# A fused attention and mixer block in fp32 by high and low parts: six plain chunks and 24 groups in place of eight and 20, with W4's low part made by DMA

## The chip, the cores and the metric

The kernel runs on one core of one Trainium2 chip. The metric is the device time of one launch in microseconds (us); the median of three runs is given, and the profile comes from one further execution. The engines are TensorE (PE), ScalarE (ACT), VectorE (DVE), GpSimd (POOL) and SyncE (SP). Each works off its own instructions in the order in which they stand and waits only by semaphores. SP and POOL issue the DMAs; in this kernel the accumulating ones (destination += source) are all issued by POOL.

## The reference, cut to what matters

```python
xn = _layernorm(x)                                  # x: 2048 tokens x 576
return x + _A_ref(xn, A_wqkv, A_wo) + _B_ref(xn, B_w1, B_w2, B_w3, B_w4)

# _A_ref: 32 heads of 18, each token sees 8 keys at distances 0, 2, .., 14
logits = einsum("bhsd,bhswd->bhsw", q, kg) * scale
o = einsum("bhsw,bhswd->bhsd", softmax(logits), vg)
return o.reshape(B, S, D) @ wo

# _B_ref: a mixer with shifted channel groups, then an MLP with F = 4608
hs = concatenate([g0, g1, g2, g3]) @ w2
x1 = x + hs
return x1 + _gelu(_layernorm(x1) @ w3) @ w4
```

All of it is float32.

## The kernel before, in words

**Precision.** A float32 operand is split into a high part, rounded to the PE's fp32r format, and a low part, the rest. A product is then three matmul passes (high x high, high x low, low x high). `PAIRS` lists the 14 passes of a 576-long contraction; `HALVES` the 7 passes of a 288-long one.

**Stages.** First qkv, spilled to DRAM (`qkvd`), then the mixer with w1 and w2, and x1 in the buffer `Y` (16 token tiles of 128 tokens). Then comes the MLP, which is two thirds of the span, and last the attention's output projection with `Wo`.

**The MLP** runs over pairs of 128-wide pieces of F. A pair is called a chunk here; there are 18.

- The first `NPL` = 8 chunks are *plain*. A unit is one chunk with one block of 512 tokens (L960): `up` makes two hidden pieces (2 x 14 matmuls of 512 columns), GELU follows on ACT, `low_part` on DVE takes the low part, and during the next unit `down` (L830) multiplies them by W4 for four token tiles (12 matmuls of 288 columns each). That is 32 units.
- The other 10 chunks run in *groups* (L1140). A group is one chunk with 1024 tokens. The two halves of the contraction, of the tokens and of the chunk form a 2 x 2 matrix product which is made with seven products (`P1` to `P7`, 7 x 7 matmuls of 512 columns) out of sums of the operands and weights. Beside the products stand eight token tiles of `down`, `D0` to `D7`, which belong to the group before. The order of these 15 items is written out by hand (`ORDER`, L1135, with other orders for the first group and for the two at the passage between the first and the second half of the tokens, `q = NWP - 1` and `q = NWP`). `at(item, f)` puts side work behind an item. There are 20 groups; group 0 also finishes the downs of the last unit.

**What a product waits for.** The products of one group share a few PSUM banks: a bank `ca` is copied by ACT after P1 (`keep(Z1, ca)`), continues to accumulate with P6, is copied again (`keep(Z2, ca)`), continues with P7 and so on (L1262 to L1286). PE may not write on before ACT's copy is done.

**Weights of a group.** `load_pair` (L915) loads w3's raw pieces into one buffer `w3st` with six DMAs; `split_a` writes the pieces for three products into `w3a`, `combine` forms sums in `w3st`, and `split_s` writes those for the other four into `w3s`. Each `split` has two ACT passes, one small accumulating DMA on POOL and one DVE pass. The next `load_pair` can start only when all readers of `w3st` are done.

**Weights W4.** `load_w4` (L554) loads 256 rows raw into the slots of token tiles 1 and 3 of `Y`. `split_w4` (L562) makes the high part on ACT (L566) and the low part on DVE (L569). Two such tiles exist.

**Token sums.** A `down` result is added to its token tile. For the ten tiles in `YD` (L34) the sum lies in DRAM: ACT copies PSUM into a staging buffer (L846) and POOL issues an accumulating DMA (L847). Their slots in `Y` are free for other use (staging, scratch, raw weights). For the other six DVE adds in `Y` (L851).

**The operands of the groups** are sums and differences of blocks of the normalised x1, loaded with `get_op` and split with `split_op` (three ACT passes L902 to L904, two DVE passes). At the passage between the token halves all seven are loaded and split anew.

**The attention** itself (scores, softmax, weighted sum) runs on DVE in the background. It is a Python generator that yields a cost after each instruction; `bg` takes pieces from it: 9.4 us per unit from unit 4 on, and in a group 1.6 us per item less what `spent` counts for other DVE work. The heads are cut into eight parts. A part's output is summed in the first half of the buffer `po` and stored to DRAM (`od`, L719). All must be done at item P4 of the sixth group from the end, where its memory is given up.

Of the kernel before, what the change touches and what calls it, by code (L numbers as in the profile page):

```python
# [17 lines left out]
NT = S // 128  # L18
# [15 lines left out]
YD = (1, 2, 3, 5, 7, 9, 10, 11, 13, 15)  # L34


NPL = 8
# [20 lines left out]
def fused_block(ctx, tc, x, wqkv, wo, w1, w2, w3, w4, out):  # L58
# [511 lines left out]

    x1n = {}
# [105 lines left out]
    def attention(ap):  # L677
# [8 lines left out]
        o = po[:, 0, :].rearrange("p (x d) -> p x d", d=HD)  # L686
# [12 lines left out]
        def av(g):  # L699
            if g == NG - 1:  # L700
                exp_now()
            L, v = Ls[g], vs[g]
            Lf = L.rearrange("p j h w -> p (j h) w")
            dve.tensor_reduce(den[g], Lf, axis=AX.X, op=ALU.add)
            dve.reciprocal(den[g], den[g])
            yield 0.8
            dve.tensor_tensor(Lf, Lf, den[g][:, :, None].to_broadcast([128, TPP * GH, W]),
                              op=ALU.mult)
            yield 0.6
            for w in range(W):  # L710
                vv = v[:, DIL * w:DIL * w + TPP, :].rearrange("p j (h d) -> p (j h) d", d=HD)
                dst = prod if w else o
                dve.tensor_tensor(dst, vv, Lf[:, :, w:w + 1].to_broadcast([128, TPP * GH, HD]),  # L713
                                  op=ALU.mult)
# [4 lines left out]
            sp.dma_start(od.rearrange("(p j) d -> p j d", p=128)[:, :, g * GC:(g + 1) * GC],  # L719
                         po[:, 0, :].rearrange("p (j c) -> p j c", c=GC))  # L720
# [242 lines left out]
    RATE = [9.4, 0.0]  # L963
# [6 lines left out]
    for u, (c, b) in enumerate(units):  # L970
# [6 lines left out]
        z = u - NU  # L977
        if z == -2:
            rtemps[:] = [2, 13, 15]
        r = 0.0 if u < 4 else (RATE[0] if z < -2 else RATE[1]) / 6  # L980
        for i in range(C):
# [11 lines left out]
            if (u, i) == (3, 0):  # L993
                pool.dma_start(yd[13], Y[:, 13, :])
                pool.dma_start(yd[15], Y[:, 15, :])
# [15 lines left out]
        for j, (t, parts) in enumerate(prev):  # L1011
# [24 lines left out]
        if z == -5:  # L1036
            load_pair(0)
        if z == -3:
# [5 lines left out]
        if z == -2:  # L1044
# [10 lines left out]
        if 14 <= u < 14 + NT:  # L1055
            add_x(u - 14)
# [83 lines left out]
    for q in range(NQ):  # L1140
# [4 lines left out]
        if q == 0:  # L1145
            rtemps[:] = [2]
        if z == -1:
            evc_pool.__exit__(None, None, None)
            opc.__exit__(None, None, None)
            EV[0] = (9, 11, 10, 2)  # L1150
# [26 lines left out]
        if q == 0:  # L1177
            at("P2", split_op, 0, "B22")
            at("P5", split_op, 0, "T4")
            at("P7", split_a, n, (0, 1))  # L1180
            at("D1", gelu22)
            at("D1", split_a, n, (2,))
            at("D2", low22)
            at("P3", combine, n)
# [4 lines left out]
            at("D3", split_w4, p)  # L1189
            at("D3", load_pair, q + 2)  # L1190
        elif q == NWP - 1:
            rtemps[:] = [2, 13]
# [10 lines left out]
            at("D2", split_w4, p)  # L1203
# [3 lines left out]
        elif q == NWP:  # L1207
            rtemps[:] = [2]
# [12 lines left out]
        elif z < -1:  # L1221
# [4 lines left out]
            at("D3", split_w4, p, 0)  # L1226
            at("P4", gelu22)
            at("P4", split_w4, p, 1)
# [7 lines left out]
        else:  # L1236
            at("D3", split_w4, p)
# [23 lines left out]
        for it in ORDERS.get(q, ORDER).split():  # L1261
# [29 lines left out]
            if z < -6 or z == -6 and EV[0]:  # L1291
                bg(1.6 - spent[0], it == "P6" and q != NWP - 1)
# [21 lines left out]
    for j in range(8):  # L1314
        tiles[j]()
        if j == 0:
            low_part(h21, Z4)
            load_y((1, 2, 3, 5))
            EV[0] = (9, 11, 10, 15, 13)
# [15 lines left out]
    for t in range(NT):  # L1335
# [6 lines left out]
        if t == 3:  # L1342
            load_y((9, 10, 11, 13, 15))
# [48 lines left out]
```

## Time and profile before

| what | us |
|---|---|
| median of 3 runs | 1292.73 (1290.86 to 1295.98) |
| profiled execution, its own time | 1294.18 |
| its span | 1292.4 |
| PE busy | 1267.1 |
| DVE busy | 944.7 |
| ACT busy | 598.7 |
| POOL busy | 246.3 |

Busy time is a sum over instructions; issuing a DMA from SP is not counted. The span by stages: from 399.6 to 718.6 us the plain units from the eighth on run, from there to about 1215 the groups, then the last downs and the output projection. In rows of waits, "A <- B: total, times, longest" is the time that A stood because B was not done. In rows of a timeline, the first two numbers are start and length in us, and the bracket at the end is the idle time before and what ended it.

### The profile page before, as it was taken

What the parts mean: (1) busy time and instruction counts of PE and PEld (TensorE: products, weight loads), DVE (VectorE), ACT (ScalarE), POOL (GpSimd) and SP (SyncE); (2) the same over time, 40 slices, a digit from 0 to 9 for tenths busy, and PEclk for the clock granted to TensorE, in tenths of its full rate; (3) what the DMA queues carried; (4) which work ended last, traced back from release to release, by engine and by line L of the source; (5) the groups of instructions that cost most, each with busy time, mean ns of one, the idle gap of its engine ahead of it and who ended that gap; (6) DMA issues with size and microseconds to landing.
All of it is one profiled execution on the core that took longest, in us unless ns stands there. A gap on an engine that the chain in (4) does not pass through costs nothing.

```text
span 1292.4 us, 19686 instructions
## 1 busy us (share of the span) xinstructions
PE 1267.1 (98%) x7538; PEld 1163.1 (90%) x7538; DVE 944.7 (73%) x1261; ACT 598.7 (46%) x952; POOL 246.3 (19%) x358
## 2 busy tenths in 40 slices
PE   8999999999999999999999999999979999999999
PEld 8999998899898998999999799989968999988998
DVE  6456534778469999999999789989978554566542
ACT  3322126526634434343345746546547555555530
POOL 2011100021221212231212212222212222222100
PEclk9999999999999999999999999999989999999999
DMA  7646874246886878989788767686595757799972
GB/s 210 156 113 139 171 173 143 73 131 174 220 245 148 180 165 202 229 154 222 136 200 204 168 136 163 112 191 154 106 261 87 155 102 154 178 218 222 254 250 83
DMA packets 201374, 219.16 MB, mean 170 GB/s; under 512 B 79152, under 2 KB 137744, under 8 KB 201152
## 3 DMA queue, kind: packets, MB, share of 16 engines
q1 hardware_dynamic: 168912, 151.57, 40.9%
q0 software_dynamic: 32368, 66.34, 32.2%
q8 instruction: 59, 0.97, 0.3%
q14 instruction: 35, 0.29, 0.1%
HBM read 119.73 MB, written 107.28 MB: 176 GB/s over the span
## 4 chain that ended last, share of the span: by engine, by line
PE 74%; DMA 8%; issue 7%; DVE 6%; ACT 2%; SPq 2%; POOL 1%; DVEq 0%; POOLq 0%; ACTq 0%
PE ps L842 26%; PE ps L214 16%; PE cc L1075 12%; PE p L823 12%; PE ps L466 4%; PE ps L313 3%; DMA yd<-Y 2%; DMA w3st<-in_B_w_dram 1%; DMA Y<-in_B_w_dram 1%; DMA w3a<-w3st 1%; DVE w L569 1%; DMA od<-po 1%; PE ps L481 1%; DVE w3st L931 1%; DMA w3s<-w3st 1%
## 5 line engine op out<-in xcount | busy, mean ns | idle before, releaser
L842 PEld LDWEIGHTS ps<-w,c 128*128 128x128 f32 x3456 | 474.9, 188 | 28.1 <-DVE Y L851 7.7
L842 PE MATMUL ps<-w,c 128*128 128x288 f32 x3456 | 486.4, 295 | 11.9 <-DVE Y L851 5.6
L847 POOL DMA_DIRECT2D yd<-Y x154 | 137.3, 897 | 453.9 <-ACT Y L846 378.6
L846 ACT COPY Y<-ps 128x576 f32<-128x576 f32 x154 | 98.1, 637 | 141.8 <-PE ps L842 90.4
L817 DVE TENSOR_TENSOR c<-Y,c 128x512 fp32r<-128x512 f32 x144 | 98.5, 685 | 60.0 <-ACT Y L806 49.9
L214 PE MATMUL ps<-WQ,xt 128*128 128x432 f32 x672 | 134.8, 360 | 0.0
L214 PEld LDWEIGHTS ps<-WQ,xt 128*128 128x128 f32 x672 | 125.6, 188 | 5.7
L851 DVE TENSOR_TENSOR Y<-ps,Y 128x576 f32<-128x576 f32 x108 | 81.1, 751 | 48.8 <-PE ps L842 48.5
L1075 PE MATMUL cc<-xt,w3s 128*128 128x512 f32 x420 | 108.8, 400 | 0.0
L737 DVE TENSOR_TENSOR po<-q,k 128x2304 f32<-128x2304 f32 (+1 forms) x40 | 82.9, 2073 | 16.1 <-issue 10.9
L805 ACT ACTIVATE c<-p 128x512 fp32r<-128x512 f32 x64 | 38.3, 599 | 119.3 <-PE p L823 119.3
L1075 PEld LDWEIGHTS cc<-xt,w3s 128*128 128x128 f32 x420 | 77.4, 192 | 14.1 <-DVE Y L1085 0.2
L740 DVE TENSOR_REDUCE L<-po 128x128 f32<-128x2304 f32 (+1 forms) x40 | 82.7, 2068 | 0.4
L1081 ACT COPY Y<-cc 128x512 f32<-128x512 f32 x60 | 35.1, 585 | 100.7 <-PE cc L1075 94.9
L121 POOL TENSOR_TENSOR rs<-rs,mhalf 128x1 f32<-128x1 f32 x48 | 31.6, 659 | 258.1 <-DVE rs L120 147.8
L717 DVE TENSOR_TENSOR po<-po 128x1152 f32<-128x1152 f32 x56 | 75.8, 1353 | 0.9
L713 DVE TENSOR_TENSOR po<-v,L 128x1152 f32<-128x1152 f32 x56 | 75.6, 1352 | 0.7
L323 ACT COPY stg<-ps 128x864 f32<-128x864 f32 x24 | 21.2, 882 | 102.8 <-PE ps L214 55.8
L1075 PE MATMUL cc<-x1n,w3a 128*128 128x512 f32 (+1 forms) x280 | 67.9, 393 | 0.0
L1075 PEld LDWEIGHTS cc<-x1n,w3a 128*128 128x128 f32 (+1 forms) x280 | 51.6, 188 | 10.3
L214 PE MATMUL ps<-W,h 128*128 128x288 f32 x384 | 53.5, 295 | 0.0
L823 PE MATMUL p<-xt,w3s 128*128 128x512 f32 x224 | 52.4, 390 | 0.0
(189 smaller groups left out, 1904.3 us busy)
## 6 DMA issues: line engine op xcount, KB each, us to landing
yd<-Y POOLq DMA_DIRECT2D x156, 288.0 KB, 5.3
Y<-in_B_w_dram SPq DMA_DIRECT2D x27, 576.0 KB, 6.9
w3st<-in_B_w_dram SPq DMA_DIRECT2D x52, 256.0 KB, 6.4
qkvd<-stg SPq DMA_DIRECT2D x24, 432.0 KB, 3.5
yd<-ev POOLq DMA_DIRECT2D x26, 288.0 KB, 6.2
xd<-st SPq DMA_DIRECT2D x16, 320.0 KB, 6.0
xd<-big SPq DMA_DIRECT2D x16, 320.0 KB, 7.9
w3st<-in_B_w_dram SPq DMA_DIRECT2D x76, 64.0 KB, 6.6
```

The source lines that it names most:

```text
L214: pe.matmul(ps[:, h, :n], xs(a), ws(b, h), start=i == 0, stop=i == len(PAIRS) - 1)
L713: dve.tensor_tensor(dst, vv, Lf[:, :, w:w + 1].to_broadcast([128, TPP * GH, HD]), op=ALU.mult)
L717: dve.tensor_tensor(o, o, dst, op=ALU.add)
L737: dve.tensor_tensor(dst, qf[:, None, :].to_broadcast([128, n, TPP * GC]), win, op=ALU.mult)
L740: dve.tensor_reduce(Lw[:, w:w + n, :], dst.rearrange("p w (x d) -> p w x d", d=HD), axis=AX.X, op=ALU.add)
L817: dve.tensor_tensor(h[:, 1, :], g, h[:, 0, :].bitcast(F32), op=ALU.subtract)
L823: pe.matmul(ps, W3[f][:, w, :], x1n[b][:, a, :], start=n == 0, stop=n == len(PAIRS) - 1)
L842: pe.matmul(ps[:, k, :HF], h[:, col], w[:, p, k * HF:(k + 1) * HF], start=n == 0, stop=n == len(seq) - 1)
L846: act.copy(e.rearrange("p (h c) -> p h c", h=2), ps[:, :, :HF])
L847: pool.dma_start(yd[t], e, accum_op=ALU.add)
L851: dve.tensor_tensor(yv, ps[:, :, :HF], yv, op=ALU.add)
L1075: pe.matmul(ps, WX[w][:k, v, SLOT[w], :], area[sb][xk][:k, a, :], start=onto is None and i == 0, stop=last and i == len(HALVES) - 1, skip_ ...
```

## The change

Six things change together; nothing that is computed does.

1. `NPL` is 6: 24 units and 24 groups.
2. `YD` has twelve tiles: 6 and 14 are summed in DRAM too. Their slots become scratch (6) and a further staging buffer (14).
3. In groups, and for the first group's W4, `split_w4g` takes the place of `split_w4`. ACT writes the negated raw value, rounded, into the low part's place; an accumulating DMA on POOL, within SBUF, adds the raw value; a second ACT pass writes the high part. DVE has no part in it.
4. The first group's W4 is loaded at the end of the fourth unit from the end of the plain stage and split in the unit after it. Before, it was loaded at the end of the second from the end and split at D3 of group 0.
5. In group 0, `split_a` of the next weights goes from behind P7 to behind P1, `combine` from P3 to D2.
6. The last of the attention's eight parts puts its output into the buffer of its q. The background budget in groups is 1.45 us per item and the rate in one late unit 5.0; x is added to the tiles seven units earlier.

```diff
-YD = (1, 2, 3, 5, 7, 9, 10, 11, 13, 15)
-NPL = 8
+YD = (1, 2, 3, 5, 6, 7, 9, 10, 11, 13, 14, 15)
+NPL = 6
...
+    def split_w4g(c, step=None):
+        t = W4["pair", c]
+        raw = Y[:, 0:4, :].rearrange("p (a b) c -> p a b c", b=2)[:, :, 1, :]
+        if step != 1:
+            act.activation(t[:, :, 1, :], raw, AF.Identity, scale=-1.0)
+            pool.dma_start(t[:, :, 1, :].bitcast(F32), raw, accum_op=ALU.add)
+        if step != 0:
+            act.copy(t[:, :, 0, :], raw)
...
+            o, out = (o_, po[:, 0, :]) if g < NG - 1 else (
+                qs[g].rearrange("p j (h d) -> p (j h) d", d=HD), qs[g].rearrange("p j d -> p (j d)"))
...
-    RATE = [9.4, 0.0]
+    RATE = [9.4, 5.0, 0.0]
+    BUDGET = 1.45
...
+        if u == 4:
+            EV[0] = (9, 11, 10, 14)
         if z == -2:
-            rtemps[:] = [2, 13, 15]
-        r = 0.0 if u < 4 else (RATE[0] if z < -2 else RATE[1]) / 6
+            rtemps[:] = [2, 6, 13, 15]
+        r = 0.0 if u < 4 else (RATE[0] if z < -3 else RATE[1] if z < -2 else RATE[2]) / 6
...
-            for f in {(-3, 1): (lambda: split_a(0),), (-3, 3): (lambda: combine(0),),
+            for f in {(-3, 1): (lambda: split_a(0),), (-3, 2): (lambda: split_w4g(NPL),), (-3, 3): (lambda: combine(0),),
...
+        if z == -4:
+            load_w4(NPL)
...
-            load_w4(NPL)
...
-        if 13 <= u < 13 + NT:
-            load_xa(u - 13)
+        if 6 <= u < 6 + NT:
+            load_xa(u - 6)
...
         if q == 0:
+            at("P1", split_a, n, (0, 1))
             at("P2", split_op, 0, "B22")
+            at("P6", split_a, n, (2,))
             at("P5", split_op, 0, "T4")
-            at("P7", split_a, n, (0, 1))
             at("D1", gelu22)
-            at("D1", split_a, n, (2,))
             at("D2", low22)
-            at("P3", combine, n)
+            at("D2", combine, n)
...
-            at("D3", split_w4, p)
...
-            at("D2", split_w4, p)
+            at("D2", split_w4g, p)
...
-            at("D3", split_w4, p, 0)
+            at("D3", split_w4g, p, 0)
             at("P4", gelu22)
-            at("P4", split_w4, p, 1)
+            at("P4", split_w4g, p, 1)
...
-            at("D3", split_w4, p)
+            at("P7", split_w4g, p)
...
-                bg(1.6 - spent[0], it == "P6" and q != NWP - 1)
+                bg(BUDGET - spent[0], it == "P6" and q != NWP - 1)
```

Three places in the engines' orders. The first is ACT in group 0, from the copy after P1 (`Y<-cc`, the buffer Z1) on. The xt rows are the split of operand B22, the second `Y<-cc` is the copy after P6, c the GELU of the next hidden piece; w3a comes from the buffer `w3st`. Before:

```order
L1081 COPY Y<-cc_6674 128x512
L902 ACTIVATE xt<-xt 128x1024
L903 ACTIVATE Y<-xt 32x512
L904 ACTIVATE xt<-xt 64x512
L1081 COPY Y<-cc_6674 128x512
L811 ACTIVATE c_6735<-Y 128x512
```

And with the change:

```order
L1097 COPY Y<-cc_5809 128x512
L947 CAST w3a<-w3st 128x768
L949 ACTIVATE w3a<-w3st,kv 96x384
L913 ACTIVATE xt<-xt 128x1024
L914 ACTIVATE Y<-xt 32x512
L915 ACTIVATE xt<-xt 64x512
L1097 COPY Y<-cc_5809 128x512
```

The two passes that write w3a stood behind the third copy of the bank; they now stand ahead of the second.

The second place is POOL's queue over one group of the first token half (yd are the stores of token tiles, w3a and w3s the small DMAs of the splits, w the low part of W4). Before:

```order
L847 DMA yd_86<-Y 128x576
L847 DMA yd_87<-Y 128x576
L847 DMA yd_88<-Y 128x576
L847 DMA yd_89<-Y 128x576
L939 DMA w3a<-w3st 32x384
L847 DMA yd_90<-Y 128x576
L939 DMA w3s<-w3st 32x512
```

And with the change:

```order
L858 DMA yd_86<-Y 128x576
L858 DMA yd_87<-Y 128x576
L858 DMA yd_88<-Y 128x576
L858 DMA yd_89<-Y 128x576
L950 DMA w3a<-w3st 32x384
L858 DMA yd_90<-Y 128x576
L858 DMA yd_91<-Y 128x576
L576 DMA w_6205<-Y 128x2x576
L950 DMA w3s<-w3st 32x512
```

A sixth tile and the whole low part of W4 stand ahead of the small DMA that ends the reading of `w3st`.

The third is ACT at the passage between the token halves (group `NWP - 1`), from the split of the second operand (x1n) to the copy of tile D3 (`Y<-ps`) and the first splits after it. Before:

```order
L902 ACTIVATE x1n_6402<-x1n_6402 128x1024
L903 ACTIVATE Y<-x1n_6402 32x512
L904 ACTIVATE x1n_6402<-x1n_6402 64x512
L566 CAST w_8665<-Y 128x2x576
L846 COPY Y<-ps_8810 128x576
L811 ACTIVATE c_8825<-Y 128x512
```

And with the change:

```order
L857 COPY Y<-ps_8393 128x576
L913 ACTIVATE x1n_5537<-x1n_5537 128x1024
L914 ACTIVATE Y<-x1n_5537 32x512
L915 ACTIVATE x1n_5537<-x1n_5537 64x512
L575 ACTIVATE w_8270<-Y 128x2x576
L578 CAST w_8270<-Y 128x2x576
L857 COPY Y<-ps_8416 128x576
```

The copy of D2 (the first row) is new, since tile 6 is now summed in DRAM, and W4 has two passes there.

More of the change, by code (lines that the diff above doesn't have):

```diff
@@ L719, in av @@
             sp.dma_start(od.rearrange("(p j) d -> p j d", p=128)[:, :, g * GC:(g + 1) * GC],
-                         po[:, 0, :].rearrange("p (j c) -> p j c", c=GC))
+                         out.rearrange("p (j c) -> p j c", c=GC))
         yield None
@@ L994, in fused_block @@
                 pool.dma_start(yd[13], Y[:, 13, :])
+                pool.dma_start(yd[14], Y[:, 14, :])
                 pool.dma_start(yd[15], Y[:, 15, :])
@@ L1145, in fused_block @@
         if q == 0:
-            rtemps[:] = [2]
+            rtemps[:] = [2, 6]
         if z == -1:
@@ L1207, in fused_block @@
         elif q == NWP:
-            rtemps[:] = [2]
             at("D1", split_op, 1, "T3")
@@ L1317, in fused_block @@
             low_part(h21, Z4)
-            load_y((1, 2, 3, 5))
-            EV[0] = (9, 11, 10, 15, 13)
+            load_y((1, 2, 3, 5, 6))
+            EV[0] = (9, 11, 10, 15, 13, 14)
         if j in (0, 2):
@@ L1342, in fused_block @@
         if t == 3:
-            load_y((9, 10, 11, 13, 15))
+            load_y((9, 10, 11, 13, 14, 15))
         if t in (5, 6):
```

9 lines of the change are left out of this document (4 added, 5 removed).

## The prediction, made before the changed kernel was run

> **What bounds the kernel now.** I read the page's first lines, then what TensorE (PE) waited for, then the chain of waits, then PE's timeline at the places named there.
>
> ```profile
> PE 1267.1 (98%) x7538; PEld 1163.1 (90%) x7538; DVE 944.7 (73%) x1261; ACT 598.7 (46%) x952; POOL 246.3 (19%) x358
> PE cc L1075 <- ACT Y L1081: 6.3, 1, 6.3
> PE ps L842 <- DVE Y L851: 5.6, 8, 1.2
> PE ps L842 <- ACT w L566: 2.0, 1, 2.0
> PE ps L842 <- DVE w L569: 0.9, 1, 0.9
> ```
>
> PE is busy 98% of the span, so 25.3 us of idle time is all there is outside its matmuls. Some 15 us of waiting have names: one of 6.3 us behind a ScalarE (ACT) copy of a product, eight short ones on VectorE (DVE) evictions, and 2.0 + 0.9 us on the split of W4. The matmuls themselves cost this, by pieces of the chain and one undisturbed group:
>
> ```profile
> 405.92 6.34 PE ps L842 x48
> 412.26 6.38 PE p L823 x28
> 785.91:809.97 24.06, 24.06 (x148) 21.94 (x147) 21.66 (x29) 16.30 (x24) 5.96 (x7) 1.00 0.80 195
> 736.29 3.39 PE L1075 MATMUL cc<-x1n,w3a 128*128 128x512 f32 x14
> 741.68 0.53 PE L842 MATMUL ps<-w,c 128*128 128x288 f32 x2 [2.00 <-ACT w L566]
> 743.07 2.77 PE L842 MATMUL ps<-w,c 128*128 128x288 f32 x10 [0.86 <-DVE w L569]
> 766.45 3.39 PE L1075 MATMUL cc<-x1n,w3a 128*128 128x512 f32 x14
> 743.07:749.90 6.83, 6.83 (x25) 6.15 (x26) 6.51 (x7) 0.60 (x2) 0.00 (x0) 0.56 0.89 225
> ```
>
> A plain unit takes 6.34 + 6.38 = 12.72 us, a group 24.06 us (columns of a windows row: stretch, then PE, PEld, DVE, ACT and POOL busy, granted clock, DMA share, GB/s). Group 1 ran from 736.29 to 766.45: 30.16 us, 6.1 more than a group. Only 2.86 of that is the wait; in the 6.83 us behind it the granted clock was 0.56, which is some 3 us more. A wait of this length so costs about its double. The second place is where the groups pass from the first half of the tokens to the second:
>
> ```profile
> 936.59 3.40 PE L1075 MATMUL cc<-x1n,w3a 128*128 128x512 f32 x14
> 974.66 0.63 PE L1075 MATMUL cc<-x1n,w3a 128*128 128x512 f32 x2
> 948.92 1.36 DVE L713 TENSOR_TENSOR po<-k,L 128x1152 f32<-128x1152 f32 x1 [7.60 <-DMA od<-po]
> 761.85 4.76 PE ps L842 x36
> 766.62 3.23 PE cc L1075 x14
> ```
>
> Between 936.59 and 974.66 lie 38.07 us. PE's work there is 7 products of 1.62 (3.23 for two) and 10 token tiles of 1.59 (4.76 for three): 27.2 us. So 10.9 us are lost, and what came first is DVE: 7.60 us behind the store of the seventh attention output, before it could write the last one into the same buffer.
>
> **Part by part, what is removed.** Two chunks less in the plain stage are 8 units of 12.72 = 101.8 us; in their place stand 4 groups of 24.06 = 96.2. That is **-5.5 us**, the only certain term. W4 for the first group is now loaded and split four units earlier, so the wait of group 1 goes: **-6.1**. What hides the split now: its two ACT passes and its DMA lie three units ahead of the groups, and the first token tile that reads this W4 stands in group 1.
>
> The last attention output goes into q's buffer, so DVE no longer waits 7.60 us. But the passage keeps seven operand splits on ACT, and W4's split there takes two ACT passes now. I take ACT's queue (shown above with the change) by these rows:
>
> ```profile
> 720.44 0.59 ACT L1081 COPY Y<-cc 128x512 f32<-128x512 f32 x1 [0.94 <-PE cc L1075]
> 720.92 1.06 ACT L902 ACTIVATE xt<-xt 128x1024 fp32r<-128x1024 f32 x1
> 722.01 0.63 ACT L903 ACTIVATE Y<-xt 32x512 fp32r<-32x512 f32 x1
> 722.66 0.63 ACT L904 ACTIVATE xt<-xt 64x512 fp32r<-64x512 f32 x1
> L566 ACT CAST w<-Y 128x1152 fp32r<-128x1152 f32 x27 | 31.2, 1157 | 20.2 <-DMA Y<-in_B_w_dram 20.2
> L846 ACT COPY Y<-ps 128x576 f32<-128x576 f32 x154 | 98.1, 637 | 141.8 <-PE ps L842 90.4
> ```
>
> One operand split is 1.06 + 0.63 + 0.63 = 2.3 us, the two W4 passes 2 x 1.16 = 2.3, a tile's copy 0.64. Behind the copy of D2 stand 4.6 us of ACT work before the copy of D3; PE needs D3's bank again after two tiles (3.2 us) less the copies, so it waits about 3 us at D5, then 1.1 at D7 and 1.3 at the next D1 behind further splits: 5.4 us, and some 1.5 of lost clock. I put the loss at 6.9 instead of 10.9: **-4.0**. Bounds: 0 (the loads of the operands set the pace) and -10.9 (all hidden).
>
> The Trainium skill, "TensorE: Matmul & The Clock Gate", Part 1, says that the clock drops to half after an idle window of about 3.4 us. Here 2.00 and 0.86 us, with two matmuls between, were enough for the 0.56 above, so the row decides; by the page the 3 us wait would cost no clock, and this term would be -5.5.
>
> Short waits on DVE: W4's low part leaves DVE 21 times, and 36 evictions go to ACT.
>
> ```profile
> L569 DVE TENSOR_TENSOR w<-Y,w 128x1152 fp32r<-128x1152 f32 x27 | 36.5, 1351 | 3.6 <-ACT w L566 3.6
> L851 DVE TENSOR_TENSOR Y<-ps,Y 128x576 f32<-128x576 f32 x108 | 81.1, 751 | 48.8 <-PE ps L842 48.5
> ```
>
> That is 21 x 1.35 + 36 x 0.75 = 55 us of DVE, 2.1 us in a group. The four extra groups bring combines, splits and sums back, off the path. DVE is what PE waited for in the eight short waits (5.6 us); I take **-4.0** (bounds 0 and -5.6). The attention's smaller budget per item costs nothing: it ends within the same group counted from the end.
>
> **What is added.** First a wait. In group 0 the cast of the next w3a now stands in ACT's queue right behind the first product's copy. It waits for this load:
>
> ```profile
> 717.28 0.78 POOL L939 DMA_DIRECT2D w3s<-w3st  x1 [9.67 <-ACT w3s L938]
> 721.02 2.56 SPq L923 DMA_DIRECT2D w3st<-in_B_w_dram  x4
> 721.61 7.62 DMA w3st<-in_B_w_dram
> 726.68 1.77 PE L1075 MATMUL cc<-x1n,w3s 128*128 128x512 f32 x7
> 729.68 0.83 ACT L936 CAST w3a<-w3st 128x768 fp32r<-128x768 f32 x1
> 730.41 0.62 ACT L938 ACTIVATE w3a<-w3st,kv 96x384 fp32r<-96x384 f32 x1
> DMA to landing us min/median/max: 4.5/6.6/11.2
> ```
>
> SyncE (SP) cannot start the load earlier, since its one buffer is read by the w3s DMA that GpSimd (POOL) issued at 717.28, and that stays where it is. It landed at 721.61 + 7.62 = 729.2; before, ACT came to it only at 729.68. Now ACT is free for it at 721.0 and stands. Behind it in order: w3a (0.83 + 0.62), operand B22 (2.3), then the copy of the second accumulation (0.59), without which PE cannot start the third product on that bank, at 726.68 in this trace. From 729.2 that is 733.6: a wait of 6.9 us; the first two of six parts land sooner, so I take 6.0, and 2.5 of lost clock: **+8.5**. Bounds +4.9 (the last part, issued at 723.6, lands in the 4.5 us of the quickest of its line, the last row: 728.1, the first pass already done by then, and no clock is lost) and +10.3 (6.9 + 3.4).
>
> Second, the DMA engines. Twelve instead of ten tiles are 36 more accumulating stores, and W4's low part is 23 accumulates of 576 KB within SBUF, a kind the trace does not have.
>
> ```profile
> q0 software_dynamic: 32368, 66.34, 32.2%
> td0T<-td0T POOLq DMA_DIRECT2D x2, 576.0 KB, 6.8
> 1043.80:1067.90 24.10, 24.10 (x146) 21.95 (x146) 12.16 (x17) 13.23 (x22) 6.03 (x8) 1.00 0.66 124
> 526.80:539.50 12.70, 12.70 (x78) 11.57 (x78) 12.70 (x10) 3.46 (x6) 4.17 (x5) 1.00 1.11 298
> 1140.10:1164.10 24.00, 23.16 (x139) 20.81 (x138) 14.13 (x23) 12.52 (x20) 5.28 (x7) 1.00 0.93 213
> 1188.20:1212.20 24.00, 24.00 (x145) 21.88 (x146) 11.91 (x18) 10.07 (x17) 5.15 (x6) 1.00 0.99 250
> ```
>
> q0 took 32.2% of 1292.4 us for 66.34 MB: 6.3 us of all engines per MB, so 1.85 us for a tile of 0.295 MB and 3.7 for a W4 low part of 0.59 MB. A group gets 5.5 us more, a share of 0.23. In quiet groups 0.66 becomes 0.89, where the low part lands in some 7 us like the DRAM accumulate of the same size. From its place at D3 to the next group's D0 lie eight pieces of 1.6 us, 12.8, less 1.2 for ACT's pass: it is there in time and costs nothing. In the last four groups 0.93 to 0.99 becomes 1.16 to 1.22, over the 1.11 that is the most any unit reached; there and in groups that load attention tiles ACT will stand some time for w3st and W4. I take **+5** over all (bounds 0: all stays hidden as in the plain stage at 1.11; +18: rival one).
>
> The Trainium skill, "DMA: Bandwidth & Descriptors", Anatomy of one DMA — SWDGE (gpsimd) path, gives 2.0 us plus bytes / 436e3 for a POOL-issued DMA, an estimate of 3.4 us for the low part; the 6.8 us row is of the same size and decides. By the page this term would be nearer its lower end.
>
> **Sum:** -5.5 - 6.1 - 4.0 - 4.0 + 8.5 + 5 = -6.1 us. The profiled execution's own time was 1294.18 (span 1292.4), so 1288.1; it lay 1.45 above the median of 1292.73, so the median should be **1286.6**.
>
> **Rivals.** *One, the DMA engines become the bound (slower).* Over 1.11 the last four groups cannot do their transfers in time: 0.05 + 0.05 + 0.11 + 0.11 of 24.06 = 7.7 us late. The loads of w3st and W4 are then late for ACT at D1 and D3, and PE with it. By the rates in the code (9.4 a unit, some 44 for one of the eight parts of the attention) 4 of these parts run beside groups, before 2.5; with two bouts of loads each that is eight bouts instead of five, and one of them already cost:
>
> ```profile
> 860.86 3.44 PE L842 MATMUL ps<-w,c 128*128 128x288 f32 x24 [1.15 <-DVE Y L851]
> ```
>
> Eight of 1.15 are 9 us, one drop of the clock 3 more: 20 in place of 5, so 1302. It decides once a group's share passes 1.1. For it: 0.99 in the last groups already. Against: at 1.11 the plain stage lost nothing. The Trainium skill, "DMA: Bandwidth & Descriptors", SWDGE vs HWDGE vs iDMA, says that an engine takes turns between POOL's and SP's queues, which would make the accumulates delay just these loads; no row here shows the turns. *Two, clean passage:* w3st lands early or ACT finds the slack, and the 10.9 us vanish: -5.5 - 6.1 - 10.9 - 5.6 + 4.9 + 2 = -21.2, so 1271. Against: ACT's order at both places. *Three, nothing is won:* the operand loads pace the passage (0 instead of -4.0), group 0 costs 10.3, DVE's short waits stay: -5.5 - 6.1 + 10.3 + 5 = +3.7, so 1296.
>
> **How the numbers follow.** Forecast 0.47 (its own range 1281 to 1292), rival one 0.26, two 0.14, three 0.13. 0.5%, about what a measurement here can tell from no change, is 6.5 us: under 1286.3 or over 1299.2. Faster: 0.28 of the forecast and 0.14 of rival two, 0.42. Within: 0.19 and 0.09 of rival three, 0.28. Slower: rival one and 0.04 of three, 0.30. The range 1272 to 1303 leaves out the far ends of rivals one and two.
>
> **What would show it.** A PE wait of 5 to 7 us before the third product of group 0 and a granted clock near half behind it; no wait on W4 in group 1; 5 to 9 us lost at the passage, with DVE not waiting for od; DMA share near 1.1 from the fifth-last group on, and short PE waits there. I am wrong if group 0 runs without a wait, or if groups in the middle take over 25 us each, which would say that W4's low part comes late.

## The result, and the profile after

The changed kernel takes 1339.86 us (median of 6 runs, 1337.89 to 1348.7) against 1292.2 of the kernel before: ratio 1.0371, 95% interval 1.0336 to 1.0405. The prediction was 1286.6, with a range up to 1303. The profiled span grew from 1292.4 to 1338.8 us, by 46.4.

From the first part of the page after, and its queues:

```profile
PE 1279.0 (96%) x7510; PEld 1170.7 (87%) x7510; DVE 915.7 (68%) x1234; ACT 661.0 (49%) x1037; POOL 317.8 (24%) x428
q0 software_dynamic: 44560, 91.87, 42.1%
```

DVE lost 29 us of work, as meant; ACT and POOL took up 62 and 72. Idle time outside PE's matmuls grew from 25 to 60 us, and the waits of PE say on what (total, times, longest):

```profile
PE cc L1091 <- ACT Y L1097: 17.9, 8, 6.9
PE ps L853 <- DMA w<-Y: 15.6, 6, 4.8
PE ps L853 <- ACT Y L857: 9.9, 4, 3.8
PE ps L853 <- DVE Y L862: 5.4, 5, 2.8
```

The second row is W4's low part, which I had in time. The first and third are ACT's copies, late because ACT itself stood for loads of w3st (before: 4.7 us in all) and for staging buffers whose stores had not landed (before: 11.4):

```profile
ACT Y L857 <- DMA yd<-Y: 39.7, 14, 6.2
ACT w3a L947 <- DMA w3st<-in_B_w_dram: 33.1, 17, 7.6
```

Stage by stage, first before, then after (first token half, passage, the quiet groups of the second half, the groups in which the attention's output is brought back; the last three columns are granted clock, DMA share and GB/s):

```profile
718.60:936.60 218.00, 213.99 (x1260) 193.50 (x1259) 197.48 (x219) 127.31 (x196) 51.74 (x62) 0.98 0.71 146
936.60:995.50 58.90, 51.35 (x293) 45.55 (x291) 45.85 (x54) 37.32 (x58) 10.28 (x13) 0.94 0.78 172
995.50:1091.70 96.20, 96.20 (x582) 87.71 (x581) 56.66 (x75) 52.87 (x84) 23.81 (x29) 1.00 0.69 135
1091.70:1191.40 99.70, 97.06 (x582) 87.86 (x581) 59.83 (x98) 53.83 (x84) 23.74 (x28) 1.00 0.90 205
```

```profile
628.80:880.50 251.70, 239.90 (x1404) 216.22 (x1404) 199.59 (x219) 154.94 (x236) 79.80 (x89) 0.98 0.88 175
880.50:968.10 87.60, 76.39 (x436) 68.94 (x436) 64.06 (x75) 57.78 (x87) 21.77 (x25) 0.96 0.86 187
968.10:1116.00 147.90, 145.52 (x873) 131.86 (x872) 125.22 (x140) 92.82 (x141) 48.88 (x54) 1.00 0.94 184
1116.00:1229.50 113.50, 102.77 (x582) 91.78 (x582) 52.80 (x90) 59.29 (x92) 30.24 (x34) 0.95 0.97 207
```

(The second stretch after has one ordinary group more, 25.3 us, ahead of the passage.) The DMA engines' share rose in all of them, by 0.25 in the groups that had been quiet and in which the attention now still runs. By first products of the groups, the 46.4 us are: plain stage +11.9 (the first group starts at 628.8 us, while before, less the 101.8 us of eight units, it would be 616.9), four groups for eight units -5.5, group 0 +10.7, group 1 -6.1, the other groups of the first half +6.3, passage +3.5, second half +17.3, tail (from the last first product to the end) +8.4. Of the plain stage's 11.9, 2.6 are lost early, behind the wait at 373.90 that is shown in the last section, and 9.3 in its last two units.

How one group loses time is seen near the end, in the timelines of ACT, POOL and PE (start, length):

```profile
1161.08 1.17 ACT L575 ACTIVATE w<-Y 128x1152 fp32r<-128x1152 f32 x1
...
1161.54 0.88 POOL L858 DMA_DIRECT2D yd<-ev  x1 [1.61 <-ACT ev L857]
1168.91 1.23 POOL L576 DMA_DIRECT2D w<-Y  x1 [6.48 <-ACT Y L823]
1169.64 1.33 POOL L950 DMA_DIRECT2D w3s<-w3st  x1
...
1175.52 2.00 PE L853 MATMUL ps<-w,c 128*128 128x288 f32 x10 [1.92 <-DMA w<-Y]
1177.32 2.97 PE L1091 MATMUL cc<-xt,w3s 128*128 128x512 f32 x7
```

ACT's pass ended at 1161.08 + 1.17 = 1162.25; POOL issued the accumulate 6.66 us later. The releaser named in the bracket is only the last event before it; an experiment below says what POOL waited for. The transfer lands after the first token tile has begun to need it. Right behind it stands the small DMA of w3s, which ends the reading of w3st. Its landing, in the view of DMA issues, before and after:

```profile
w3s<-w3st POOLq DMA_DIRECT2D x19, 64.0 KB, 2.5
```

```profile
w<-Y POOLq DMA_DIRECT2D x23, 576.0 KB, 5.7
...
w3s<-w3st POOLq DMA_DIRECT2D x23, 64.0 KB, 4.7
```

So the next load of w3st can only start later, ACT stands at its cast, and the product's copy behind it comes late. This is one path among several: in m1 below the w3s DMA lands in 2.5 us again, and ACT still waits 30.5 us for loads of w3st (L947, here 33.1).

### The profile page after: what moved, and what is told of

The parts are those of the page before. It is cut to its first block, busy times and chain, and to the rows that moved or that the text cites. A ratio compares the mean times of both kernels' runs of the same rounds, so it can differ in the third digit from the quotient of the medians.

```text
span 1338.8 us, 19925 instructions
## 1 busy us (share of the span) xinstructions
PE 1279.0 (96%) x7510; PEld 1170.7 (87%) x7510; DVE 915.7 (68%) x1234; ACT 661.0 (49%) x1037; POOL 317.8 (24%) x428
## 3 DMA queue, kind: packets, MB, share of 16 engines
q0 software_dynamic: 44560, 91.87, 42.1%
## 4 chain that ended last, share of the span: by engine, by line
PE 58%; DMA 19%; issue 10%; DVE 5%; ACT 3%; SPq 3%; POOL 2%; POOLq 0%; DVEq 0%; ACTq 0%
PE ps L853 18%; PE ps L214 15%; PE p L834 9%; PE cc L1091 8%; DMA w3st<-in_B_w_dram 6%; PE ps L466 4%; PE ps L313 3%; DMA w3s<-w3st 3%; DMA x1n<-xn 1%; DMA yd<-Y 1%; DMA w3a<-w3st 1%; POOL yd L858 1%; DMA xt<-xd 1%; DMA xn<-st 1%; DMA xt<-xn 1%
## 5 line engine op out<-in xcount | busy, mean ns | idle before, releaser
L853 PEld LDWEIGHTS ps<-w,c 128*128 128x128 f32 x3456 | 486.1, 192 | 50.8 <-DMA w<-Y 17.0
L853 PE MATMUL ps<-w,c 128*128 128x288 f32 x3456 | 499.3, 299 | 32.1 <-DMA w<-Y 15.6
L858 POOL DMA_DIRECT2D yd<-Y x186 | 169.4, 951 | 358.5 <-ACT Y L857 246.7
L857 ACT COPY Y<-ps 128x576 f32<-128x576 f32 x186 | 117.9, 635 | 137.5 <-PE ps L853 93.4
L1091 PE MATMUL cc<-xt,w3s 128*128 128x512 f32 (+1 forms) x504 | 130.9, 400 | 1.4 <-DVE Y L1101 1.4
L1091 PEld LDWEIGHTS cc<-xt,w3s 128*128 128x128 f32 (+1 forms) x504 | 92.9, 192 | 18.2 <-DVE Y L1101 1.6
L1091 PE MATMUL cc<-x1n,w3a 128*128 128x512 f32 (+1 forms) x336 | 82.2, 395 | 0.0
L1101 DVE TENSOR_TENSOR Y<-cc,Y 128x512 f32<-128x512 f32 x72 | 49.4, 686 | 42.7 <-ACT Y L1097 35.6
L942 DVE TENSOR_TENSOR w3st<-w3st 128x384 f32<-128x384 f32 x92 | 51.3, 557 | 33.8 <-issue 15.8
L862 DVE TENSOR_TENSOR Y<-ps,Y 128x576 f32<-128x576 f32 x72 | 54.1, 751 | 20.7 <-PE ps L853 20.5
```

Of the source, the lines that this page charges most:

```text
L853: pe.matmul(ps[:, k, :HF], h[:, col], w[:, p, k * HF:(k + 1) * HF], start=n == 0, stop=n == len(seq) - 1)
L857: act.copy(e.rearrange("p (h c) -> p h c", h=2), ps[:, :, :HF])
L858: pool.dma_start(yd[t], e, accum_op=ALU.add)
L862: dve.tensor_tensor(yv, ps[:, :, :HF], yv, op=ALU.add)
L1091: pe.matmul(ps, WX[w][:k, v, SLOT[w], :], area[sb][xk][:k, a, :], start=onto is None and i == 0, stop=last and i == len(HALVES) - 1, skip_ ...
```

## The experiments

Each is compared with the kernel before on the same chip (its median was 1293.5 to 1295.5 us, and 1292.2 beside the changed kernel). "Changed" is the changed kernel, 1339.9. It was not run again beside the experiments, so a difference between two of these times carries some 3 us from one comparison to the next. Many of the kernels also have a budget of their own for the attention, and the budget is not neutral: see g1 below.

**W4's low part and the two tiles, undone singly and together.**

```diff
-            at("D3", split_w4g, p, 0)
+            at("D3", split_w4, p, 0)
...
-BUDGET = 1.45
+BUDGET = 1.55
```

> The changed kernel with W4's low part made by DVE again (split_w4 in all groups and for the first group's W4, at the same places; background budget 1.55 per item so that the attention still ends at the same item). Theory Q (POOL's queue: the 24 accumulates of 576 KB push the small stores and themselves late): the waits on the DMA of w (15.6 us in the changed kernel) are gone, with some 8 us of clock behind them, and the late copies of w3a shrink: 1339.9 less 25 = 1315, half of what the change lost. Theory S (the 36 more stores of two more token tiles fill the DMA engines, W4's DMA is only the victim): PE waits for W4 go, but ACT and DVE waits take their place: not under 1330. Theory P (the costs sit in group 0 and in the last plain units): 1325 to 1332.

```diff
-YD = (1, 2, 3, 5, 6, 7, 9, 10, 11, 13, 14, 15)
+YD = (1, 2, 3, 5, 7, 9, 10, 11, 13, 15)
...
-BUDGET = 1.45
+BUDGET = 1.5
```

> The changed kernel with the ten token tiles of before in DRAM (tiles 6 and 14 in Y again, their slots neither scratch nor staging; budget 1.5). 36 stores less on POOL's queue, q0 back by 10.6 MB. Theory Q: W4's accumulates stay and stay late: a gain of 5 to 10 only, 1330 to 1335. Theory S: the stores were what filled the engines: 1339.9 less 20 or more, 1320 or under. Theory P: within 3 of 1340.

Measured 1303.49 and 1316.14. The first is under all three expectations; the second is in theory S's, which had asked for 1330 or more in the first. So neither theory holds for both. With both edits and a budget of 1.6:

> The changed kernel with both of the earlier undoings: W4's low part by DVE and ten tiles in DRAM (budget 1.6 as before). What is left of the change: six plain chunks and 24 groups, the early first W4, the last output in q's buffer, group 0's order. The single undoings gave -36.4 and -23.7 us. Theory Q (one resource, POOL's queue, that only jams when both loads stand on it): the sum is far from additive, since the jam is nearly gone with one: 1290 to 1300. If the two costs are separate and add: 1280. By the terms of my prediction without DMA costs (-5.5, -6.1, -4.0, 0 on DVE, +8.5): 1293.5 - 7 = 1286.

1300.52, just over theory Q's range. So the two loads, with the budgets that go with them, cost 39.4 us together; W4's transfer costs 15.6 where tiles 6 and 14 stay in Y, the two tiles cost 3.0 where DVE splits W4 (no more than two comparisons can differ by), and 20.8 come only when both stand there. The costs do not add, as theory Q expected; that POOL's queue is the place is not shown by this. And the four budgets differ (1.45, 1.55, 1.5, 1.6), so 15.6, 3.0 and 20.8 are not prices of the transfers alone.

**What of W4's transfer costs.** First on ACT's own queue as a plain copy, then not at all; both kernels leave W4's low part out of the result, and change nothing else:

```diff
-            pool.dma_start(t[:, :, 1, :].bitcast(F32), raw, accum_op=ALU.add)
+            act.dma_start(t[:, :, 1, :].bitcast(F32), raw)
```

> The changed kernel with W4's low part as a plain copy within SBUF (raw over the negated high part, not added: the low part is left out of the result) issued by ACT on its own queue, right behind the pass that it overwrites. The bytes go through the DMA engines all the same; POOL's queue is rid of them, and nothing is read back for the sum. Theory R/Q (POOL's queue): near e1's 1303, at most 1310, and no PE wait on the DMA of w. Theory E (the engines' time): 1325 to 1340. In between would be the price of reading the destination.

```diff
-            pool.dma_start(t[:, :, 1, :].bitcast(F32), raw, accum_op=ALU.add)
```

> The changed kernel without the accumulating DMA of W4's low part: ACT's two passes stay, the sum is left out of the result. The plain copy on ACT's queue gave only -10.5 of the -36.4 us that DVE's split gave. Theory E (the bytes cost, whichever queue carries them): with no transfer at all the time falls to that of the DVE split or below, 1295 to 1305. Theory ACT (the second pass of 1.16 us in ACT's order is what delays the copies and the casts of w3a): it stays at 1325 to 1335.

Measured 1329.37, in theory E's range, and 1312.4, which neither expectation had. So the transfer alone, with the same budget, costs 27.5 us: 10.5 are POOL's queue and the reading of the destination, 17.0 the copy on ACT's queue, its bytes and its issue (ACT stands 0.96 us around the issue of the copy at 791.83). Of the 36.4 us that DVE's split gave back, 8.9 remain between no transfer and DVE's split. Where they lie the traces show: the fifth group from the end takes 32.2 us in m2 and 24.1 in e1. In m2 the loads of the attention's output stand ahead of w3's there, as the last rows of the next section show it for the changed kernel; m2 has the budget of 1.45, e1 1.55. So most of this part belongs to the attention's late end and not to the transfer. In m1 the copies have a queue of their own (packets, MB, share of 16 engines):

```profile
q10 hardware_dynamic: 6256, 13.57, 2.7%
```

That is 0.027 x 1330.5 / 23 = 1.56 us of all engines for a copy. An accumulate of the same bytes takes, from q0's share in the changed kernel (42.1% of 1338.8, 563.6 us) and in m2 (38.1% of 1306.8, 497.9 us), 65.7 / 23 = 2.86 us; with m1 or e1 in place of m2 it is 2.7 or 3.1.

**What POOL waits for.**

```diff
-                    dynamic_dma_scratch_size=1024)
+                    dynamic_dma_scratch_size=1408)
```

> The changed kernel with 1408 instead of 1024 bytes per partition for the descriptors of POOL's DMAs, and nothing else. The traces show POOL standing up to 10 us before it issues a store or W4's accumulate although what they read has long been there; if what it waits for is room for descriptors (theory R), 38% more room lets it run further ahead: 1339.9 less 8 to 20, and the mean idle time ahead of W4's accumulate falls from some 3.7 us. If it waits for the engines to work off what is queued (theory E), a longer queue changes nothing, or only makes the small DMAs of w3a and w3s later: 1336 to 1345.

1333.74: -6.1, less than theory R's 8 to 20. The same place as above in the timelines of ACT and POOL, and the landing:

```profile
1153.41 1.17 ACT L575 ACTIVATE w<-Y 128x1152 fp32r<-128x1152 f32 x1
...
1153.88 0.86 POOL L858 DMA_DIRECT2D yd<-ev  x1 [1.99 <-ACT ev L857]
1155.05 1.22 POOL L576 DMA_DIRECT2D w<-Y  x1 [0.30 <-issue]
...
w<-Y POOLq DMA_DIRECT2D x23, 576.0 KB, 7.3
```

Over the 23 accumulates the time from the end of ACT's pass to POOL's issue falls from 3.73 us on average to 0.47, so what POOL stood for was room for descriptors. What the text ahead of the prediction says, that an engine waits only by semaphores, misses this wait. The room is not the main cost: the transfers are issued earlier, land 7.3 instead of 5.7 us after the issue, and the group is late all the same. ACT's waits for staging buffers fall from 39.7 to 7.9 us, but PE's waits for ACT's copies (L857) rise from 9.9 to 19.2. And some 3.8 of the 6.1 us may be the shorter quiet groups of the last section (0.16 us each, 24 groups). With ten tiles the same delay is 0.63 us with 1024 bytes too: the two extra tiles are what fills the room.

**Where it costs.**

```diff
-            at("D3", split_w4g, p, 0)
+            at("D3", split_w4g if q < NWP else split_w4, p, 0)
...
-            at("D2", split_w4g, p)
+            at("D2", split_w4, p)
...
-BUDGET = 1.45
+BUDGET = 1.48
```

> The changed kernel with W4's low part by DMA only up to the passage (groups 1 to 10) and by DVE from the passage on (budget 1.48, so that the attention ends where it does in the changed kernel). If the cost is local (passage 4 to 9 us, last groups 12, tail 8): 1339.9 less 22 to 28 = 1312 to 1318. If every transfer costs alike (36.4 us over 24): 13 of 24 gone, 1320. If the end stays late because the attention ends at its limit: over 1325.

1322.7: 17.2 of 36.4 us for 12 of 23 transfers taken away, between the expectations. By the total the cost looks spread; the trace says otherwise. Where the transfers are gone, some 26 us are won, as the local theory had it (22 to 28): the passage falls from 62.4 to 52.2 us, the second half from 261.3 to 254.4 and the tail from 109.3 to 100.2, while the fifth group from the end still takes 30.2. But groups 1 to 10, whose transfers stayed, take 259.1 instead of 248.6 us, behind PE waits of 2.52, 2.83 and 1.93 us and a lower clock. The only part of the edit that acts there is the budget, 1.48 instead of 1.45. So by these traces 0.03 of budget moves 10 us, and every comparison of two budgets here must be read with that. The transfer alone in the kernel before:

```diff
-            at("D3", split_w4, p, 0)
+            at("D3", split_w4g, p, 0)
...
-                bg(1.6 - spent[0], it == "P6" and q != NWP - 1)
+                bg(1.51 - spent[0], it == "P6" and q != NWP - 1)
```

> The kernel before with one part of the change alone: W4's low part in groups by the accumulating DMA (at the change's places; budget 1.51, which leaves the attention where it was). My prediction: in quiet groups at a share of 0.66 + 0.15 it costs nothing, and frees 28 us of DVE: 1290 to 1294. Theory E (transfers jam only where the engines are near full): +4 to +12, in the last four groups and the passage: 1298 to 1306. If the accumulate itself is slow anywhere: over 1310, with lost time in quiet groups.

1304.0, ratio 1.0074 (1.0048 to 1.01). Its groups 2 to 8 stay at 24.1 to 25.4 us, the passage takes 63.9 instead of 58.9 and the tail 103.9 instead of 101.0: the loss is local, as theory E had it. At the passage DVE's wait for the store of od, which this kernel still has, grows from 7.60 to 11.30 us, and PE's one wait of 11.0 us there is for DVE. The budget (1.51) is another here too.

**Group 0.**

```diff
-            at("P1", split_a, n, (0, 1))
...
-            at("P6", split_a, n, (2,))
...
+            at("P7", split_a, n, (0, 1))
...
+            at("D1", split_a, n, (2,))
...
-            at("D2", combine, n)
+            at("P3", combine, n)
```

> The changed kernel with group 0 as before: split_a of the next weights behind P7 and D1, combine behind P3. My prediction put +8.5 on this place and the trace shows +10.7 there. If the place is a cost of its own: 1329 to 1331. If the later split_a only hands the delay on (w3st free later, load of the next weights late in group 1): 1335 to 1340.

The same edit on e5:

> As e5 (the changed kernel with W4 by DVE and ten tiles, 1300.5) and with group 0's order of before too. If that order is a cost of its own when the engines have room: 1300.5 less 6 to 8 = 1293 to 1294. If the delay is handed on as in the jammed kernel: 1298 to 1301.

In the jammed kernel 1338.21, nearly nothing: group 0 falls from 28.4 to 17.8 us in the trace, but the ten groups behind it take 5.5 us more and the tail 3.2. On e5 it is 1290.08, -10.4, of which group 0 itself is 8.2 in the traces (25.9 and 17.7). The starts of groups 0 and 1 in f1's timeline of PE, with no wait between:

```profile
623.66 3.39 PE L1090 MATMUL cc<-x1n,w3a 128*128 128x512 f32 x14
...
641.31 3.39 PE L1090 MATMUL cc<-x1n,w3a 128*128 128x512 f32 x14
```

**The end of the plain stage.**

```diff
-        if 6 <= u < 6 + NT:
-            load_xa(u - 6)
+        if 2 <= u < 2 + NT:
+            load_xa(u - 2)
-        if 7 <= u < 7 + NT:
-            add_x(u - 7)
+        if 3 <= u < 3 + NT:
+            add_x(u - 3)
```

> The changed kernel with x added to the token tiles four units earlier (from unit 2 on, done by unit 18), so that none of it stands in POOL's queue in the last plain units, where the stores waited 9.8 us behind one of these adds and the plain stage lost 12 us. If these adds are the cause there: the waits of 3.75 and 2.76 us and their clock go, 1330 to 1333. If the first W4's accumulate and the operands' loads are: 1338 to 1341, and e1 is to show the end of the plain stage clean instead.

The sums instead, in the changed kernel:

```diff
-        if 5 <= u < 21 and u % 2:
-            sums((u - 5) // 8, (u - 5) % 8 // 2)
+        if 4 <= u < 12:
+            sums((u - 4) // 4, (u - 4) % 4)
```

> The changed kernel with the eight steps of the operands' sums (16 transfers of 576 KB within DRAM) in units 4 to 11 instead of every second unit from 5 to 19. If the end of the plain stage jams by these: the waits of 3.75 and 2.76 us there go, 1339.9 less 5 to 8. If the engines are full throughout the plain stage (share 0.88 to 1.00 from 320 us on, before 0.76 to 0.89), the loss only moves to earlier units: 1337 to 1345.

Measured 1350.63 and 1362.56. Both expectations failed: nothing is gained at the end of the stage (the first group starts at 629.8 and 647.7), and moving transfers earlier makes the whole slower. That six chunks leave no units with room would explain it, but is not shown. The 12 us of the plain stage stay without one cause; with W4 on DVE and ten tiles some 6 remain (first group of e5 at 622.7).

**The attention's end.**

In the changed kernel:

```diff
-    BUDGET = 1.45
+    BUDGET = 1.6
```

> The changed kernel with the background budget of before, 1.6 us per item instead of 1.45. In the changed kernel the attention ends at its limit (last output stored at 1112.0, in the sixth group from the end; before at 1006, four groups earlier), and the loads of its outputs for the next stage start right behind that store. Theory A (the late attention costs: SP's queue holds these loads ahead of w3's in the fifth group from the end): that group goes from 29.9 back to 25, the groups behind it lose less: 1339.9 less 6 to 12. If it doesn't cost: 1337 to 1342.

In the kernel before:

```diff
-                bg(1.6 - spent[0], it == "P6" and q != NWP - 1)
+                bg(1.4 - spent[0], it == "P6" and q != NWP - 1)
```

> The kernel before with a smaller budget alone (1.4 instead of 1.6 us per item), so that its attention ends at the limit as in the changed kernel. Theory A: +5 to +12, lost in the five or six groups before the end: 1299 to 1306. If the place of the attention's end does not matter: 1291 to 1296.

1340.11 and 1310.27. The first total is that of "it doesn't cost", but two effects cancel in it. In the changed kernel the earlier end gains 5.8 us in the fifth group from the end (24.1) and loses 9.8 in groups 1 to 10 (two groups of 30.0 and 31.1). In the kernel before a budget of 1.4 costs 16 us, more than the 5 to 12 expected. 8.7 of them are in the group of the limit: what is left there is put on DVE at one place, and PE waits for an eviction behind it:

```profile
1100.39 6.13 PE L842 MATMUL ps<-w,c 128*128 128x288 f32 x24 [5.79 <-DVE Y L851]
```

7.2 more are in the group ahead of it, where DVE now waits 7.15 us for the seventh store of od: that wait stood at the passage with 1.6, and moves with the budget. So the budget has a narrow best value: too high and DVE's evictions in the first half are late, too low and the rest jams at the limit.

**Two parts of the change alone in the kernel before.**

```diff
+            o, out = (o_, po[:, 0, :]) if g < NG - 1 else (
+                qs[g].rearrange("p j (h d) -> p (j h) d", d=HD), qs[g].rearrange("p j d -> p (j d)"))
...
+        if z == -4:
+            load_w4(NPL)
...
-            load_w4(NPL)
...
-            at("D3", split_w4, p)
```

> The kernel before with two parts of the change alone: the last attention output in q's buffer, and the first group's W4 loaded and split (by ACT and DVE) in the plain stage, as in the change. By my prediction's terms -4.0 at the passage and -6.1 in group 1: 1283.4 (0.992). With the whole 10.9 us of the passage: 1276.5. If the operand loads pace the passage, -6.1 alone: 1287.

b1 with a smaller budget and more descriptor room, and then with the budget alone:

```diff
-                bg(1.6 - spent[0], it == "P6" and q != NWP - 1)
+                bg(1.5 - spent[0], it == "P6" and q != NWP - 1)
...
-                    dynamic_dma_scratch_size=1024)
+                    dynamic_dma_scratch_size=1408)
```

> The kernel before with the output in q's buffer and the early first W4 (1294.3 against 1294.9), and in addition a budget of 1.5 instead of 1.6 (the attention still ends ahead of its limit) and 1408 bytes for descriptors. In b1 PE's waits on DVE evictions rose from 5.6 to 8.4 us in the groups of the first half; if that is DVE's background in the way, 1.5 takes it back: 1294 less 4 to 8, 1286 to 1290, faster than both kernels. If the operands' loads at the passage and the engines set the pace: 1292 to 1296. If the later attention costs as it did with 1.4 (1310): 1298 or more.

> f4 without the larger descriptor room (1024 bytes, as in the kernel before): output in q's buffer, early first W4, budget 1.5. If the budget made f4's gain: 1284 to 1288. If the room (or what moves with it: a quiet group of 23.9 instead of 24.06 us, some 3 us over 20 groups) made it: 1291 to 1294 and quiet groups of 24.1.

And f1 with the 1408 bytes alone:

> f1 (six plain chunks, 24 groups, W4 by DVE, ten tiles, group 0 as before, output in q's buffer, early first W4; 1290.1) with 1408 bytes for descriptors. If the room brings what it brought to the changed kernel (-6): 1284, quiet groups of 23.9. If it brings only the shorter groups (0.16 x 24): 1286. If nothing: 1289 to 1291.

b1 gains nothing: 1294.32, ratio 0.9996. Its group 1 and its passage are 3.4 and 1.8 us shorter, and other groups, one of 27.8 us, lose it again behind DVE's evictions. With a budget of 1.5 as well: f7 1283.47, ratio 0.9909 (0.9888 to 0.9929), the lowest median here. f4, with 1408 bytes in addition, has 1285.28, f6 1292.24 against f1's 1290.08 in another comparison: the room is worth nothing where POOL does not stand. The first half and the passage of f7, by the view of stretches:

```profile
720.40:932.80 212.40, 211.12 (x1259) 191.16 (x1258) 185.58 (x210) 125.97 (x195) 51.62 (x62) 1.00 0.74 150
932.80:986.40 53.60, 50.38 (x293) 45.52 (x292) 42.90 (x51) 37.62 (x58) 10.32 (x13) 0.97 0.79 178
```

218.0 and 58.9 before: 5.6 us less in the first half, where my -6.1 stood, and 5.3 less at the passage, where my -4.0 stood. But the two parts may not be what pays. These are the seventh stores of od in the kernel before, in b1 and in f7:

```profile
939.81 0.52 SPq L719 DMA_DIRECT2D od<-po  x1
940.84 0.53 SPq L721 DMA_DIRECT2D od<-po  x1
991.51 0.53 SPq L721 DMA_DIRECT2D od<-po  x1
```

In b1 the store stands at the passage, so the output in q's buffer is tried there, and it gains 1.8 us. In f7 the budget has moved the store behind the passage. In b3, with a budget of 1.4 and neither part, the passage's first group falls from 38.1 to 31.0 us and group 1 from 30.2 to 27.3. The kernel before with a budget of 1.5 alone was not run, so how much of f7's gain is the two parts and how much the budget is not shown.

## Why the prediction was wrong

- *DMA engines, +5.* This is the step that failed. The load was not too small: I put 5.5 us of engine time on a group, and q0's shares give some 4.3 (2.86 for W4's low part, and 1.46 for a tile: e2's q0, 38.5% of 1316.2, is 56.9 us lower, for 39 transfers fewer). What it costs was mis-sized: 27.5 us for W4's transfer alone by m2, and 39.4, eight times the term, for both loads with their budgets by e5. I looked for a threshold, 1.11, that a share must pass, because the plain stage had lost nothing there. The groups lose at 0.88 to 0.97. What PE waits for there are single transfers, W4's low part itself and ACT's copies behind loads of w3st and staging stores, and this shows in no mean share. The loads of w3st hardly take longer from issue to landing (6.6 and 6.7 us by size, before 6.4 and 6.6), so slower transfers are not the whole account; which delay costs how much stays open.
- "it is there in time and costs nothing" was wrong twice. I had the transfer issued as ACT's pass ends; POOL stood 3.73 us on average for descriptor room. And of a DMA put into POOL's queue I counted its own landing but not what stands behind it: the w3s DMA went from 2.5 to 4.7 us (2.5 again in m1, where POOL's queue is free of the transfer), although the order shown ahead of the prediction has it there. The sign of being wrong that I named came: five of groups 1 to 10 take over 25 us. But it does not say there that W4's low part is late: of PE's waits in these groups 0.5 us is for that, and 4.3 for ACT's copies of products.
- *Rival one* had the mechanism (loads of w3st and W4 late) and the sign, with 20 us in place of 39 and a chance of 0.26. Its condition, a share over 1.1, was not met: the last groups have 0.97.
- *The plain stage.* The prediction has no term for it, and it lost 11.9 us; 5.9 of them remain in e5, without both loads.
- *Group 0, +8.5.* Right: a wait of 6.93 us before the third product at 644.67, +10.7 in the trace, 8.2 in the traces of e5 and f1.
- *Group 1, -6.1.* Right: 24.1 us.
- *Passage, -4.0.* DVE waits there for no store of od any more, but not for the reason given: with 24 groups the seventh store falls at 1071.9, far behind the passage. And the passage takes 62.4 us instead of 58.9: PE stood 1.78 and 1.99 us for ACT's copies and then 4.81 for W4's low part, which I had not placed there. Without the transfers it is 51.7 (e5).
- *Short waits on DVE, -4.0.* Did not come: 5.4 us of such waits, before 5.6.
- *Six chunks, -5.5,* "the only certain term": the matmuls are saved, yet f1, with six chunks and none of the transfers, has 1290.1 and f7, with eight, 1283.5. The attention's work of eight units goes into groups; f1 loses 5 us more at the end of its plain stage, behind late stores, and 6 more in its first half. f1's budget is 1.6 and f7's 1.5, so this comparison has two differences.
- "The attention's smaller budget per item costs nothing: it ends within the same group counted from the end" was wrong. Before, the last store of od stands at 1006.2, three groups ahead of the limit; after, at 1112.0, at the limit. SP then works off the first loads of the output (L1139) ahead of w3's, here in its own queue's timeline:

```profile
1118.21 6.80 SPq L1139 DMA_DIRECT2D Y<-od  x12
1125.18 0.91 SPq L931 DMA_DIRECT2D w3st<-in_B_w_dram  x2
```

  and that group (P1 at 1116.0) takes 29.9 us, 24.1 with a budget of 1.6 (m3).

## What to carry to other kernels

Moving work from an engine at 73% to DMAs is not free because the engines' mean share stays under 1: ask which single transfers PE waits for, and what stands behind the new one in its queue. Price two new loads on one queue together, since here the pair cost far more than the two singly (39.4 us against 15.6 and 3.0, budgets included). When an edit is undone and a tuning value is moved along with it, the difference is not the edit's alone: 0.03 of background budget moved some 10 us, and the same two parts gave 0 with one budget and 0.9% with another. Run the value alone as well.

## What was not expected of the hardware

- An accumulating DMA within SBUF held the 16 engines 1.8 times as long as a plain copy of the same bytes (2.86 against 1.56 us for 576 KB; 1.7 to 2.0 times by the other two subtractions).
- POOL stands when the room for its descriptors is used up, and the profile shows this as idle time with an unrelated releaser; only the larger room showed it (3.73 to 0.47 us).
- What a wait costs PE beyond itself is not settled by its length. Twelve matmuls of 288 columns behind four waits, three in the changed kernel and the last in e1:

```profile
333.11 1.85 PE L853 MATMUL ps<-w,c 128*128 128x288 f32 x12 [1.05 <-ACT ev L857]
...
373.90 2.90 PE L853 MATMUL ps<-w,c 128*128 128x288 f32 x12 [2.36 <-ACT Y L857]
...
626.26 2.73 PE L853 MATMUL ps<-w,c 128*128 128x288 f32 x12 [2.76 <-DVE Y L862]
...
374.66 1.85 PE L853 MATMUL ps<-w,c 128*128 128x288 f32 x12 [2.36 <-ACT Y L857]
```

  The same 2.36 us was followed by slow matmuls once and by none once. In all the traces here, from 300 to 1230 us, 18 of 39 PE waits of 1.73 to 2.2 us were followed by a granted clock under 0.99 over the next 6.8 us, and every wait above 3.1 us was. The Trainium skill, "TensorE: Matmul & The Clock Gate", Part 1, puts the drop behind an idle window of about 3.4 us that runs free of the kernel. That it runs free fits one length with both outcomes; the drops behind 2.36 and 2.76 us come earlier than the 3.4, and there the measurement decides.
- In all three kernels with 1408 bytes a quiet group took 23.9 instead of 24.06 us; the matmuls of 512 columns with operands from xt and w3s took 389 ns on average in f6 and 394 in f1. The descriptors' room moves all buffers; that this is the cause was not tried.
